# Retention followed by a gated MLP on one core: batch 0's states formed as 128x128 products of head pairs

## The chip, the core and the metric

The kernel runs on one NeuronCore of a Trainium2 chip. Its time is the device time of one execution in microseconds (us). Engines in the profile: PE is TensorE's matrix products and PEld its weight loads, DVE is VectorE, ACT is ScalarE, POOL is GpSimd, SP is SyncE, which here only issues DMAs. The profile also tells which share of TensorE's full clock was granted at each moment.

## The reference

Eight batches of eight heads, 576 positions, head dimension 64. Each head applies decaying causal attention without a softmax; the heads are laid side by side as 512 columns and go through two matrix products with a swish between them.

```python
# attention: q, k, v are (8, 8, 576, 64)
scores = scale * np.matmul(q, k.transpose(0, 1, 3, 2))
gamma = 1.0 - 2.0 ** (-5.0 - np.arange(H))
rel = pos[:, None] - pos[None, :]
Dmat = np.where(rel >= 0, gamma[:, None, None] ** rel, 0.0)
attn_out = np.matmul(scores * Dmat[None], v)
# MLP: x is (4608, 512), w_in (512, 2048), w_out (2048, 512)
x = attn_out.transpose(0, 2, 1, 3).reshape(B * S, H * D)
h = x @ w_in
g = h * (1.0 / (1.0 + np.exp(-beta * h)))
out = g @ w_out
```

## The kernel before

The decay is split into a factor on the queries (`gq`) and one on the values (`gv`, `gvh`), so a masked product of queries and keys remains, and what lies before a chunk of positions can be summed up in a state, the product of keys and values of each head, a 64x64 matrix. The first 512 positions of each batch are one block of the MLP; the last 64 positions of all batches together make another block. A block has "ups" (16 groups `fo` of 128 hidden columns, each the sum over four 128-row slices `ko` of `w_in`, then a swish on ACT that writes `gT`) and "downs" (four row groups `ms`, each the sum over 16 slices `fo` of `w_out`). Ups and downs of one block are products of 128x128 weights with 512 columns, 64 each. They are the list `fill`; attention steps of the next batch, loads and casts are put between its entries by `merged`, by hand-written positions in `streams`. The order of instructions on every engine is the order in which the program writes them (manual schedule).

Batch 0 is different, since nothing can run before it. It is loaded first (queries, keys, values, by head halves `a` and spans `s` of 256 positions), then `w_in` in pieces, then `w_out`, all in one queue on SP. Its steps are written out by hand at lines 718 to 773:

- `warm_up(n, cols)` puts n filler products on PE, on a tile of zeros in f32. In the profile each counts as two products.
- `t_q`, `s_T`: transposes of queries and keys on PE; `pre_q` (DVE) and `pre_s` (POOL) scale and cast ahead of them, and ACT copies the transposed keys to `kT`.
- `s_sc`: scores, then the causal mask on DVE (line 487).
- `s_st(a, n, s, rows)` (line 513): products of keys and values that make a state. States 0, 1 and 2 sum up what lies before positions 128, 256 and 384; the call at `n = 2` with the `high` rows of span 1 completes the state at the end of the block. Each head has a 64x64 product of its own; a product takes `rows` of one span, state 2 starts a PSUM tile of its own and forms span 0's part again.
- `s_keep(a, n, es)` (line 526) copies a state from PSUM to bf16 in `sbds`, the block-diagonal state of head pairs, on ACT for half 0 and mostly on DVE for half 1. The final state goes to `ends`.
- `s_O`, `s_cross`, `s_x`: masked scores times values; queries times state, added to the same PSUM tiles; the copy to `xT`, the input of the ups.

After line 773 the rest of half `a = 1` (`rest`: three `s_cross`, the last state's products, two `s_x`, casts of `w_in`) follows the first entry of `fill`, and `last_state` follows the third. Casts of `w_in` go to POOL and DVE (`cast_w_in`, line 209), those of `w_out` to DVE and ACT (`cast_w_out`, line 224).

Batch 1's queries and keys are transposed on PE among block 0's downs (`t_q`, `t_k`), after DVE's `pre_q` and POOL's `pre` have prepared them; later batches use DMA transposes (`turn`, line 330).

Of the kernel before, what the change touches and what calls it, by code (L numbers as in the profile page):

```python
# [19 lines left out]
def kernel(  # L20
# [218 lines left out]
    def warm_up(n, cols=256, tag="mm"):  # L239
        ph = psum.tile([P, MB], F32, name="ph", tag=tag, bufs=3 if tag == "mm" else 1)  # L240
        for _ in range(n):
            nc.tensor.matmul(ph[:, :cols], warm[:, :P], warm[:, :cols], start=True, stop=True,  # L242
                             skip_group_check=True)

    def betas():
        pb = psum.tile([P, FO], F32, name="pb", tag="mm", bufs=3)
# [79 lines left out]
    def heads(t, p):  # L326
        return t[:, 2 * p:2 * p + 2, :].rearrange("p h d -> p (h d)")
# [116 lines left out]
    def half(x):  # L444
        return slice(x * D, (x + 1) * D)
# [67 lines left out]
    def s_st(a, n, s, rows):  # L513

        if n not in s_sts:
            t = psum.tile([P, 1 if n > 1 else 2, 2, 2, D], F32, name="st", tag="mm" if n > 1 else "st", bufs=3 if n > 1 else 1)
            s_sts.update({2: t[:, 0]} if n > 1 else {0: t[:, 0], 1: t[:, 1]})
        S = spans[s]
        for i in range(2):
            for pl in range(2):  # L520
                for j in range(2):
                    h = 2 * (2 * a + pl) + j
                    nc.tensor.matmul(s_sts[n][half(j), a, pl, :], S["kn"][rows, i, h, :], S["vn"][rows, i, h, :],
                                     start=n != 1 and a == 0 and s == 0 and i == 0 and pl == 0, stop=True, skip_group_check=True)

    def s_keep(a, n, es):

        for j in range(2):
            if n < 3:
                es[j](sbds[n][half(j), 2 * a:2 * a + 2, half(j)], s_sts[n][half(j), a])  # L530
            else:
                es[j](ends[0][half(1 - j if a else j), 2 * a:2 * a + 2], s_sts[2][half(j), a])

    def piece(u, c):

# [139 lines left out]
    def down(m, ms, f0, fn=4, n0=0, nn=d_model):  # L675

        gT = gts[m]
        if f0 == 0:
            pos_[ms] = psum.tile([P, d_model], F32, name="po", tag="mm" if m or ms < 3 else "st", bufs=3 if m or ms < 3 else 1)
        po = pos_[ms]  # L680
        for fo in range(f0, f0 + fn):
            nc.tensor.matmul(po[:, :nn], gT[:, fo, ms, :], w_out_sb[:, fo, n0:n0 + nn],  # L682
                             start=(fo == 0), stop=(fo == FO - 1))
        if f0 + fn < FO:
            return
        if m not in ots:
            ots[m] = stage.tile([P, MB // P, d_model], F32, name="ot", tag="wt", bufs=4)
        ot = ots[m][:, ms, n0:n0 + nn]
        (nc.scalar.copy if m == 0 else nc.vector.tensor_copy)(ot, po[:, :nn])  # L689
        if m < B:  # L690
            rows = out[m * S:m * S + MB].rearrange("(s i) n -> s i n", i=CB)
            if m < 2:
                held.append((rows[:, ms, n0:n0 + nn], ot))
            else:
                nc.sync.dma_start(rows[:, ms, n0:n0 + nn], ot)
        else:
            for x in range(2):
                r0 = (2 * ms + x) * S + MB
                nc.sync.dma_start(out[r0:r0 + TL, n0:n0 + nn], ot[x * TL:(x + 1) * TL])
# [12 lines left out]
    def F(f, *a):  # L712
        return lambda: f(*a)
# [1 line left out]

    whole_span, low, high = slice(0, P), half(0), half(1)

    warm_up(5)
    betas()
    betas_safe()  # L720
    pre_q(0, 0)
# [1 line left out]
    t_q(0, 0)  # L723
    pre_q(0, 2)
    pre_q(0, 3)
    warm_up(1, 128)
    t_q(0, 1)
    warm_up(2, 128)
    pre_s(0, 0, 0)
    s_T(0, 0)  # L730
    pre_s(1, 0, 0)
    warm_up(2, 128)
    s_sc(0, 0, "sc")
    s_T(1, 0)
    pre_s(0, 0, 1)
    pre_s(1, 0, 1)
    warm_up(2, 128)
    s_T(0, 1)
    s_sc(1, 0, "mm")
    pre_s(0, 1, 0)  # L740
    pre_s(1, 1, 0)
    warm_up(2, 128, "st")
    s_T(1, 1)
    s_sc(0, 1, "sc")
    pre_s(0, 1, 1)
    pre_s(1, 1, 1)
    s_st(0, 0, 0, low)
    s_st(0, 1, 0, whole_span)
    s_keep(0, 0, (act, act))
    s_keep(0, 1, (act, act))  # L750
    s_st(0, 2, 0, whole_span)
    s_O(0, 0, "O")
    s_sc(1, 1, "mm")
    s_st(0, 2, 1, low)
    s_keep(0, 2, (act, act))
    s_O(1, 0, "O")
    s_cross(1, 0)
    s_cross(2, 0)
    s_x(0, 0, act)
    s_st(1, 0, 0, low)  # L760
    s_st(1, 1, 0, whole_span)
    s_keep(1, 0, (dve, dve))
    s_keep(1, 1, (dve, dve))
    s_O(0, 1, "sc")
    s_cross(3, 0)
    s_x(0, 1, act)
    s_st(1, 2, 0, whole_span)
    s_st(1, 2, 1, low)
    s_keep(1, 2, (act, act))
    s_O(1, 1, "sc")  # L770
    cast_w_in(0, (0, 1), (1,))
# [3 lines left out]
    def rest():  # L775
        for c in range(1, CB):
            s_cross(c, 1)
        for a in range(2):
            s_st(a, 2, 1, high)
        s_x(1, 0, act)  # L780
        s_x(1, 1, dve)
        cast_w_in(1, (2, 3))
        nc.vector.reciprocal(rbeta_sb[:], beta_sb[:])

    def last_state():
        for a in range(2):
# [35 lines left out]
    def triangles():  # L822
# [3 lines left out]
        for t, pattern in zip(tri, ([[1, CB], [CB, TL // CB]], [[1, TL]])):  # L826
            nc.gpsimd.memset(t[:], 1.0)
            for x in range(2):
# [1 line left out]
                nc.gpsimd.affine_select(out=t[w], in_=t[w], pattern=pattern, compare_op=ALU.is_ge,  # L830
                                        fill=0.0, base=0, channel_multiplier=-1)

    streams = [[(d0 + 2, F(triangles)), (1, rest), (3, F(last_state))], [(0, F(load_w_out, 0)), (1.6, F(cast_w_in, 2)), (2.1, F(cast_w_in, 3)), (2.2, F(load_w_out, 1)),
                (4.1, F(cast_w_in, 4)), (6.1, F(cast_w_in, 5)), (6.2, F(load_w_out, 2)), (8.1, F(cast_w_in, 6)),
                (10.1, F(cast_w_in, 7)), (10.2, F(load_w_out, 3))],
               [(d0 - 4 + 3.3 * g, F(cast_w_out, g)) for g in range(WG)],
# [100 lines left out]
```

## Time and profile before

| what | value |
|---|---|
| times of three executions | 299.07, 301.01 and 298.75 us, median 299.07 |
| the profiled execution | 300.7 us, of which the span from first to last instruction is 299.0 |
| TensorE's clock in the span, mean share granted | 0.993 |
| PE busy | 291.1 us (97%), 3309 products |
| DVE, ACT, POOL busy | 102.3, 145.4, 110.6 us |
| DMA | 53.99 MB, mean 181 GB/s |

Times in rows are in us unless marked ns. A timeline row holds the start, the length to the end of the last of the group, engine, line, operation, tiles and count, and in brackets the idle time of the engine before it and what ended that. In a row of the table of stretches, each engine has its busy time and, in brackets, the number of instructions that began there; after them come the granted clock and the DMA share. A product's recorded length contains its passage through the array, which overlaps with the next one's; what a product costs in a row of products is the distance of starts.

### The profile page before, as it was taken

What the parts mean: (1) busy time and instruction counts of PE and PEld (TensorE: products, weight loads), DVE (VectorE), ACT (ScalarE), POOL (GpSimd) and SP (SyncE); (2) the same over time, 40 slices, a digit from 0 to 9 for tenths busy, and PEclk for the clock granted to TensorE, in tenths of its full rate; (3) what the DMA queues carried; (4) which work ended last, traced back from release to release, by engine and by line L of the source; (5) the groups of instructions that cost most, each with busy time, mean ns of one, the idle gap of its engine ahead of it and who ended that gap; (6) DMA issues with size and microseconds to landing.
All of it is one profiled execution on the core that took longest, in us unless ns stands there. A gap on an engine that the chain in (4) does not pass through costs nothing.

```text
span 299.0 us, 7758 instructions
## 1 busy us (share of the span) xinstructions
PE 291.1 (97%) x3309; PEld 150.4 (50%) x3309; DVE 102.3 (34%) x214; ACT 145.4 (49%) x255; POOL 110.6 (37%) x219
## 2 busy tenths in 40 slices
PE   7969999999999999999999999999999999999996
PEld 5734446774454454455445544454454544444444
DVE  6727444713740353025402540255055400120012
ACT  5526817695257434843475248524771157107600
POOL 5947027855642802282229424865232000000000
PEclk9979999999999999999999999999999999999999
DMA  7999999999999959994989969999896110131012
GB/s 230 308 368 330 386 235 268 214 185 251 219 205 247 230 126 146 238 198 113 206 225 227 196 115 260 197 181 203 210 198 115 72 37 0 35 72 36 0 70 72
DMA packets 124178, 53.99 MB, mean 181 GB/s; under 512 B 101856, under 2 KB 116592, under 8 KB 124144
## 3 DMA queue, kind: packets, MB, share of 16 engines
q1 hardware_dynamic: 124112, 53.49, 80.8%
q8 instruction: 26, 0.43, 0.6%
q14 instruction: 8, 0.07, 0.1%
q10 hardware_dynamic: 32, 0.01, 0.0%
HBM read 36.71 MB, written 9.44 MB: 154 GB/s over the span
## 4 chain that ended last, share of the span: by engine, by line
PE 78%; DMA 9%; SPq 7%; POOL 3%; issue 2%; DVE 1%; ACT 0%; POOLq 0%
PE po L682 36%; PE ph L649 28%; PE ph L664 4%; DMA tln<-in_k_dram 4%; SPq L123 4%; DMA qn<-in_q_dram 4%; DMA kT<-kn 2%; SPq L330 1%; POOL qs L289 1%; SPq L96 1%; PE O L608 1%; PE st L580 1%; PE O L621 1%; POOL kn L311 1%; PE sc L562 1%
## 5 line engine op out<-in xcount | busy, mean ns | idle before, releaser
L682 PE MATMUL po<-w_out_sb,gT 128*128 128x512 bf16 (+2 forms) x608 | 128.8, 368 | 0.0
L651 ACT ACTIVATE gT<-ph,beta_sb 128x512 bf16<-128x512 f32 (+1 forms) x140 | 91.1, 656 | 52.0 <-PE ph L649 51.5
L649 PE MATMUL ph<-xT,w_in_sb 128*128 128x512 bf16 (+1 forms) x560 | 115.1, 364 | 0.0
L682 PEld LDWEIGHTS <-gT 128*128 128x128 bf16 x608 | 56.8, 98 | 63.0
L649 PEld LDWEIGHTS <-w_in_sb 128*128 128x128 bf16 x560 | 54.2, 98 | 57.7 <-DVE first L588 0.7
L689 DVE COPY ot<-po 128x512 f32<-128x512 f32 (+2 forms) x34 | 22.3, 657 | 72.1 <-PE po L682 72.0
L322 POOL CAST kn<-kvn 128x128 bf16<-128x128 f32 (+2 forms) x76 | 23.4, 344 | 47.9 <-DMA kvn<-in_k_dram 47.8
L289 POOL TENSOR_TENSOR qs<-qn,gq 128x256 bf16<-128x256 f32 (+1 forms) x36 | 26.3, 757 | 34.7 <-DMA qn<-in_q_dram 32.3
L569 DVE TENSOR_TENSOR R<-sc,tri 128x512 bf16<-128x512 f32 x28 | 17.4, 683 | 61.5 <-PE sc L562 61.5
L300 POOL TENSOR_TENSOR vn<-kvn,gv 128x512 bf16<-128x512 f32 x28 | 29.1, 1042 | 7.7 <-DMA kvn<-in_v_dram 7.5
L636 ACT CAST xT<-O 128x512 bf16<-128x512 f32 x14 | 7.5, 588 | 31.9 <-PE O L621 31.9
L591 ACT CAST sbd<-warm 128x256 bf16<-128x256 f32 x18 | 7.3, 405 | 25.5 <-DVE warm L588 20.6
L664 PE MATMUL ph<-xT,w_in_sb 128*128 128x512 bf16 x56 | 13.4, 397 | 0.0
L588 DVE TENSOR_TENSOR first<-st,warm 128x256 f32<-128x256 f32 x24 | 10.2, 425 | 2.5
L588 DVE TENSOR_TENSOR warm<-st,first 128x256 f32<-128x256 f32 x18 | 7.6, 422 | 9.6 <-PE st L580 8.4
L636 DVE CAST xT<-O 128x512 bf16<-128x512 f32 x14 | 9.0, 686 | 5.4 <-PE O L621 5.4
L667 ACT ACTIVATE gT<-ph,beta_sb 128x512 bf16<-128x512 f32 x14 | 8.5, 687 | 4.3 <-PE ph L664 4.2
L310 POOL TENSOR_TENSOR kn<-tln,gq 128x128 bf16<-128x128 f32 (+1 forms) x12 | 5.6, 470 | 12.8 <-DMA tln<-in_q_dram 9.1
L214 POOL CAST w_in_sb<-wt 128x256 bf16<-128x256 f32 (+1 forms) x15 | 7.7, 528 | 5.4 <-DMA wt<-in_moe_w_in_dram 5.2
L664 PEld LDWEIGHTS <-w_in_sb 128*128 128x128 bf16 x56 | 5.4, 100 | 6.7 <-issue 0.6
L242 PE MATMUL ph<-warm 128*128 128x128 f32 (+1 forms) x28 | 7.2, 396 | 1.3 <-DVE warm L135 1.3
L591 ACT CAST sbd<-first 128x256 bf16<-128x256 f32 x18 | 7.3, 405 | 2.3 <-DVE first L588 0.2
(105 smaller groups left out, 168.2 us busy)
## 6 DMA issues: line engine op xcount, KB each, us to landing
qn<-in_q_dram SPq DMA_DIRECT2D x16, 512.0 KB, 5.3
kvn<-in_k_dram SPq DMA_DIRECT2D x32, 256.0 KB, 5.9
kvn<-in_v_dram SPq DMA_DIRECT2D x32, 256.0 KB, 5.4
out_dram<-ot SPq DMA_DIRECT2D x31, 256.0 KB, 3.7
wt<-in_moe_w_out_dram SPq DMA_DIRECT2D x8, 512.0 KB, 7.4
wt<-in_moe_w_in_dram SPq DMA_DIRECT2D x5, 512.0 KB, 9.4
wt<-in_moe_w_in_dram SPq DMA_DIRECT2D x6, 256.0 KB, 6.9
out_dram<-ot SPq DMA_DIRECT2D x9, 128.0 KB, 2.4
```

The source lines that it names most:

```text
L289: nc.gpsimd.tensor_tensor(batch[b]["qs"][:, cs, to], q_tiles[b][:, hs, cs].rearrange("p h i d -> p i h d"), gq[:, cs, hs].unsqueeze(3).to_ ...
L300: nc.gpsimd.tensor_tensor(live[i]["vn"], kv_tiles.pop(i)[:, 1], gains(gv, c), ALU.mult)
L322: nc.gpsimd.tensor_copy(kn[:, c % 2, to], t[:, 0, hs])
L569: nc.vector.tensor_tensor(R[x][:, j].rearrange("k c p q -> k (c p) q"), sc[x, j].rearrange("k c p q -> k (c p) q"), mask, ALU.mult)
L588: nc.vector.tensor_tensor(new[:], add, sums[(c - 1) % 2][:], ALU.add)
L591: nc.scalar.copy((sbq[c] if c < NC - 1 else ends[u])[:], new[:])
L636: (nc.scalar.copy if n % 2 else nc.vector.tensor_copy)(x, o)
L649: nc.tensor.matmul(ph, w_in_sb[:, ko, fo * P:(fo + 1) * P], xts[m][:, ko, :, w], start=(ko == 0), stop=(ko == KO - 1))
L651: nc.scalar.activation(gts[m][:, fo, :, w], ph, ACT.Silu, scale=beta_sb[:, fo:fo + 1])
L664: nc.tensor.matmul(phs[f][:], w_in_sb[:, ko, f * P:(f + 1) * P], xts[m][:, ko], start=(ko == 0), stop=(ko == KO - 1))
L682: nc.tensor.matmul(po[:, :nn], gT[:, fo, ms, :], w_out_sb[:, fo, n0:n0 + nn], start=(fo == 0), stop=(fo == FO - 1))
L689: (nc.scalar.copy if m == 0 else nc.vector.tensor_copy)(ot, po[:, :nn])
```

## The change

- `warm_up` gains a form with 512 columns; the opening five fillers of 256 columns become two of 512 and one of 256.
- The nine later fillers (f32, 128 columns, at five places and one single) become five calls of `keep_warm`, one bf16 product of 512 columns each, of the identity with itself.
- `s_st` makes one 128x128 product for a pair of heads in place of two 64x64 ones; `s_keep` copies the two diagonal 64x64 squares out. States 1, 2 and the end of the block now grow in one PSUM tile (`s_sts[1]`): span 0 is taken in whole once, state 1 is copied, then span 1's low rows are added, state 2 is copied, then the high rows are added. State 0 keeps the tile tagged `st`. The call for state 1 now stands ahead of that for state 0.
- The last products move out of `rest` into `last_products` at position 2.5 of `fill`, and `last_state` moves from 3 to 3.6.
- In `down`, block 0's products from `fo` = 3 on are made as two products of 256 columns.

```diff
--- before.py
+++ after.py
@@ -239,8 +239,14 @@
     def warm_up(n, cols=256, tag="mm"):
         ph = psum.tile([P, MB], F32, name="ph", tag=tag, bufs=3 if tag == "mm" else 1)
         for _ in range(n):
-            nc.tensor.matmul(ph[:, :cols], warm[:, :P], warm[:, :cols], start=True, stop=True,
+            src = warm[:].unsqueeze(1).to_broadcast([P, 2, 256]) if cols > 256 else warm[:, :cols]
+            nc.tensor.matmul(ph[:, :cols], warm[:, :P], src, start=True, stop=True,
                              skip_group_check=True)
+
+    def keep_warm(tag="mm"):
+        ph = psum.tile([P, CB, P], F32, name="ph", tag=tag, bufs=3 if tag == "mm" else 1)
+        nc.tensor.matmul(ph[:], ident[:], ident[:].unsqueeze(1).to_broadcast([P, CB, P]), start=True, stop=True,
+                         skip_group_check=True)
 
     def betas():
         pb = psum.tile([P, FO], F32, name="pb", tag="mm", bufs=3)
@@ -513,23 +519,22 @@
     def s_st(a, n, s, rows):
 
         if n not in s_sts:
-            t = psum.tile([P, 1 if n > 1 else 2, 2, 2, D], F32, name="st", tag="mm" if n > 1 else "st", bufs=3 if n > 1 else 1)
-            s_sts.update({2: t[:, 0]} if n > 1 else {0: t[:, 0], 1: t[:, 1]})
+            s_sts[n] = psum.tile([P, HP, P], F32, name="st", tag="mm" if n else "st", bufs=3 if n else 1)
         S = spans[s]
         for i in range(2):
-            for pl in range(2):
-                for j in range(2):
-                    h = 2 * (2 * a + pl) + j
-                    nc.tensor.matmul(s_sts[n][half(j), a, pl, :], S["kn"][rows, i, h, :], S["vn"][rows, i, h, :],
-                                     start=n != 1 and a == 0 and s == 0 and i == 0 and pl == 0, stop=True, skip_group_check=True)
+            for p in (2 * a, 2 * a + 1):
+                nc.tensor.matmul(s_sts[n][:, p, :], heads(S["kn"][rows, i], p), heads(S["vn"][rows, i], p),
+                                 start=a == 0 and s == 0 and i == 0 and p == 0, stop=True, skip_group_check=True)
 
     def s_keep(a, n, es):
 
+        ps = slice(2 * a, 2 * a + 2)
         for j in range(2):
+            st = s_sts[min(n, 1)][half(j), ps, half(j)]
             if n < 3:
-                es[j](sbds[n][half(j), 2 * a:2 * a + 2, half(j)], s_sts[n][half(j), a])
+                es[j](sbds[n][half(j), ps, half(j)], st)
             else:
-                es[j](ends[0][half(1 - j if a else j), 2 * a:2 * a + 2], s_sts[2][half(j), a])
+                es[j](ends[0][half(1 - j if a else j), ps], st)
 
     def piece(u, c):
 
@@ -679,8 +684,10 @@
             pos_[ms] = psum.tile([P, d_model], F32, name="po", tag="mm" if m or ms < 3 else "st", bufs=3 if m or ms < 3 else 1)
         po = pos_[ms]
         for fo in range(f0, f0 + fn):
-            nc.tensor.matmul(po[:, :nn], gT[:, fo, ms, :], w_out_sb[:, fo, n0:n0 + nn],
-                             start=(fo == 0), stop=(fo == FO - 1))
+            parts = ((0, nn),) if m or fo < 3 else ((0, nn // 2), (nn // 2, nn))
+            for x, y in parts:
+                nc.tensor.matmul(po[:, x:y], gT[:, fo, ms, :], w_out_sb[:, fo, n0 + x:n0 + y],
+                                 start=(fo == 0), stop=(fo == FO - 1), skip_group_check=m == 0)
         if f0 + fn < FO:
             return
         if m not in ots:
@@ -715,7 +722,8 @@
 
     whole_span, low, high = slice(0, P), half(0), half(1)
 
-    warm_up(5)
+    warm_up(2, MB)
+    warm_up(1)
     betas()
     betas_safe()
     pre_q(0, 0)
@@ -723,49 +731,47 @@
     t_q(0, 0)
     pre_q(0, 2)
     pre_q(0, 3)
-    warm_up(1, 128)
+    keep_warm()
     t_q(0, 1)
-    warm_up(2, 128)
+    keep_warm()
     pre_s(0, 0, 0)
     s_T(0, 0)
     pre_s(1, 0, 0)
-    warm_up(2, 128)
+    keep_warm()
     s_sc(0, 0, "sc")
     s_T(1, 0)
     pre_s(0, 0, 1)
     pre_s(1, 0, 1)
-    warm_up(2, 128)
+    keep_warm()
     s_T(0, 1)
     s_sc(1, 0, "mm")
     pre_s(0, 1, 0)
     pre_s(1, 1, 0)
-    warm_up(2, 128, "st")
+    keep_warm("st")
     s_T(1, 1)
     s_sc(0, 1, "sc")
     pre_s(0, 1, 1)
     pre_s(1, 1, 1)
+    s_st(0, 1, 0, whole_span)
+    s_keep(0, 1, (act, act))
     s_st(0, 0, 0, low)
-    s_st(0, 1, 0, whole_span)
     s_keep(0, 0, (act, act))
-    s_keep(0, 1, (act, act))
-    s_st(0, 2, 0, whole_span)
     s_O(0, 0, "O")
     s_sc(1, 1, "mm")
-    s_st(0, 2, 1, low)
+    s_st(0, 1, 1, low)
     s_keep(0, 2, (act, act))
     s_O(1, 0, "O")
     s_cross(1, 0)
     s_cross(2, 0)
     s_x(0, 0, act)
+    s_st(1, 1, 0, whole_span)
+    s_keep(1, 1, (dve, dve))
     s_st(1, 0, 0, low)
-    s_st(1, 1, 0, whole_span)
     s_keep(1, 0, (dve, dve))
-    s_keep(1, 1, (dve, dve))
     s_O(0, 1, "sc")
     s_cross(3, 0)
     s_x(0, 1, act)
-    s_st(1, 2, 0, whole_span)
-    s_st(1, 2, 1, low)
+    s_st(1, 1, 1, low)
     s_keep(1, 2, (act, act))
     s_O(1, 1, "sc")
     cast_w_in(0, (0, 1), (1,))
@@ -775,12 +781,14 @@
     def rest():
         for c in range(1, CB):
             s_cross(c, 1)
-        for a in range(2):
-            s_st(a, 2, 1, high)
         s_x(1, 0, act)
         s_x(1, 1, dve)
         cast_w_in(1, (2, 3))
         nc.vector.reciprocal(rbeta_sb[:], beta_sb[:])
+
+    def last_products():
+        for a in range(2):
+            s_st(a, 1, 1, high)
 
     def last_state():
         for a in range(2):
@@ -830,7 +838,7 @@
                 nc.gpsimd.affine_select(out=t[w], in_=t[w], pattern=pattern, compare_op=ALU.is_ge,
                                         fill=0.0, base=0, channel_multiplier=-1)
 
-    streams = [[(d0 + 2, F(triangles)), (1, rest), (3, F(last_state))], [(0, F(load_w_out, 0)), (1.6, F(cast_w_in, 2)), (2.1, F(cast_w_in, 3)), (2.2, F(load_w_out, 1)),
+    streams = [[(d0 + 2, F(triangles)), (1, rest), (2.5, F(last_products)), (3.6, F(last_state))], [(0, F(load_w_out, 0)), (1.6, F(cast_w_in, 2)), (2.1, F(cast_w_in, 3)), (2.2, F(load_w_out, 1)),
                 (4.1, F(cast_w_in, 4)), (6.1, F(cast_w_in, 5)), (6.2, F(load_w_out, 2)), (8.1, F(cast_w_in, 6)),
                 (10.1, F(cast_w_in, 7)), (10.2, F(load_w_out, 3))],
                [(d0 - 4 + 3.3 * g, F(cast_w_out, g)) for g in range(WG)],
```

## The prediction

> **What bounds the kernel now.** I read the page first, then the waits of PE, a table of stretches, and the timelines of the first 60 us.
>
> ```profile
> PE 291.1 (97%) x3309; PEld 150.4 (50%) x3309; DVE 102.3 (34%) x214; ACT 145.4 (49%) x255; POOL 110.6 (37%) x219
> PEclk9979999999999999999999999999999999999999
> q8 instruction: 26, 0.43, 0.6%
> ...
> PE O L498 <- issue: 2.4, 1, 2.4
> PE sc L562 <- DMA kT<-kn: 0.3, 1, 0.3
> ...
> 177.46 0.70 DVE ot L689
> 225.31 4.87 DMA kT<-kn
> ```
>
> PE is busy 97% of the span, so time can come from three places only: fewer or cheaper products, PE's idle time, or its clock. Of the idle time one wait stands out: 2.4 us before line 498, put down to "issue", which is a wait that the profile cannot name. The clock row dips in one slice, the one from 15 to 22 us. The chain that ended last runs over DMAs between 177 and 225 us, but it gets there from an output copy behind PE's downs, and PE waited only 0.3 us at its end: that stretch moves with PE.
>
> ```profile
> 14.81 0.41 PE L498 MATMUL O<-R,vn 64*64 64x128 bf16 x14
> 17.62 0.24 PE L498 MATMUL O<-R,vn 64*64 64x128 bf16 x2 [2.40 <-issue]
> 19.04 1.89 PE L664 MATMUL ph<-xT,w_in_sb 128*128 128x512 bf16 x4
> 20.72 0.85 PE L506 MATMUL O<-qT,sbd 128*128 128x128 bf16 x6
> ...
> 0.00:12.12 12.12, 9.92 (x94) 7.67 (x94) 7.40 (x23) 6.28 (x11) 8.39 (x26) 1.00 0.93 253
> 0.00:15.22 15.22, 13.02 (x223) 10.14 (x223) 10.50 (x28) 9.01 (x19) 11.39 (x31) 1.00 0.97 271
> 18.20:21.60 3.40, 3.40 (x46) 1.89 (x42) 0.00 (x0) 1.23 (x4) 1.61 (x5) 0.50 1.08 385
> ...
> q8 instruction: 1, 0.02, 6.0%
> ```
>
> The gap lies inside one group: 14 of 16 like products run, two come 2.4 us later, with operands long there. I read it as a wait for PE's own program. The page's queue q8 moved 26 packets, 0.43 MB, so 16.5 KB each; PE ran 3309 products and 3309 weight loads, 6618 instructions, 255 for a packet. The last row is the DMA view of 15.0 to 16.2 us, with the first packet of all; to 15 us there is none. At 15.22 us, 223 products and as many loads had begun: 446 instructions. So PE began with two packets in hand less some 66 instructions of start-up (2 x 256 - 446), and asked for the third on entering the second, at instruction 190, product 95. By the row to 12.12 us, 94 had begun by then. From 12.1 to 17.6 us the packet took **5.5 us**, on DMA engines at a share of 0.93 to 1.08. PE used the 256 instructions in 3.1 us, and stood still for the rest.
>
> The clock follows: from 18.2 to 21.6 us the granted share is 0.50. Four products of 512 columns take 1.68 us there (19.04 to 20.72), 0.42 each. The stretch costs half of 3.4 us, 1.7. That also sorts the times shown: 301.01 and the profiled 300.7 lie 1.6 to 2.3 above 299.07 and 298.75, the size of one such stretch. I take it that the wait is in every execution and the half clock in some.
>
> **The change, part by part.**
>
> ```profile
> L242 PE MATMUL ph<-warm 128*128 128x128 f32 (+1 forms) x28 | 7.2, 396 | 1.3 <-DVE warm L135 1.3
> L523 PE MATMUL st<-vn,kn 64*64 64x64 bf16 (+1 forms) x80 | 2.7, 203 | 0.0
> 7.92 0.66 PE L242 MATMUL ph<-warm 128*128 128x128 f32 x4
> 8.42 0.39 PE L468 MATMUL T<-ident,kn 128*128 128x128 bf16 x4
> 12.37 0.66 PE L523 MATMUL st<-vn,kn 64*64 64x64 bf16 x24
> 12.96 0.42 PE L498 MATMUL O<-R,vn 64*64 64x128 bf16 x16
> 50.02 0.40 PE L431 MATMUL st<-vn,kn 128*128 128x128 bf16 x4
> 50.26 1.03 PE L682 MATMUL po<-w_out_sb,gT 128*128 128x512 bf16 x4
> ```
>
> *The wait.* Fillers fall from 28 counted products to 11 (two of 512 and one of 256 columns count double, five single), states from 80 to 32. In the new order the 95th product is in the first state call and the 223rd in `last_products`, behind 12 products of 512 columns and six `s_cross`. I put the ask at 12.2 us, so the packet is there at 17.7, and the 223rd due near 19.2 (below). The wait goes: **-2.4**. Bounds: 0 if the packet is as late again as it was needed, -2.4 if it is early. I take the end, with 1.5 us of margin.
>
> *The half clock.* PE has no gap over a microsecond left, so the stretch should not recur: **-1.7** in an execution that had it, 0 in one that had not.
>
> *State products.* Before, 24 took 0.59 us (12.37 to 12.96). Whole pairs cost what line 431 shows, four in 0.24. The 32 new ones then cost 1.9 us and the 80 old ones 2.0: nothing on PE, and a gain in instructions alone.
>
> *Fillers.* An f32 four cost 0.50 (7.92 to 8.42); a bf16 one of 512 columns 0.22 (27.96 less 26.23 over eight, in rows further down). The five places fall from 2.1 to 1.1 us, but PE is paced by others there.
>
> ```profile
> 10.02 5.05 DVE L487 TENSOR_TENSOR R<-sc,causal 128x512 bf16<-128x512 f32 x8 [1.20 <-PE sc L484]
> 14.98 1.21 DVE L530 CAST sbd<-st 64x128 bf16<-64x128 f32 x4
> 11.00 2.04 POOL L461 TENSOR_TENSOR vn<-kvn,gvh 128x512 bf16<-128x512 f32 x2
> 14.64 0.58 ACT L510 CAST xT<-O 128x512 bf16<-128x512 f32 x1
> ```
>
> POOL's values of span 0 end near 12.04 whatever PE does, and eight masks run on DVE without a break. Only their start comes earlier, by the 0.25 that the first filler gives up before `s_T(0, 0)`: the masks end at 14.8 in place of 15.07.
>
> *The new wait.* State 2 is now added into the tile that `s_keep(1, 1)` reads, on DVE behind the masks: two copies of 0.3 end at 15.4. PE waits 0.7 us ahead of that product, and `s_O(1, 1)` and the first ups stand behind it, until 15.7 and 15.95. Without the program wait the old order would have had its ups at 16.2, behind ACT's `xT` copy (0.58, after the `s_cross` at 15.4). So the wait hides behind what was there, and a net **-0.15** remains. Bounds: -0.4, +0.7.
>
> *What the ups then meet.* First ups 15.95; `s_cross` to 17.2; second ups to 18.0; their `xT` half at 18.05; third ups to 19.0; last products 0.45; fourth to 20.3; eight more products to 22.0; 8 (lines 649) to 23.7; the 32 of line 664 follow. All need weights:
>
> ```profile
> 22.22 0.75 POOL L214 CAST w_in_sb<-wt 128x512 bf16<-128x512 f32 x1 [0.60 <-DMA wt<-in_moe_w_in_dram]
> 23.77 0.61 POOL L214 CAST w_in_sb<-wt 128x512 bf16<-128x512 f32 x1 [0.80 <-DMA wt<-in_moe_w_in_dram]
> 25.02 2.18 POOL L214 CAST w_in_sb<-wt 128x512 bf16<-128x512 f32 x2 [0.64 <-DMA wt<-in_moe_w_in_dram]
> 26.23 1.89 PE L649 MATMUL ph<-xT,w_in_sb 128*128 128x512 bf16 x8
> 27.96 7.07 PE L664 MATMUL ph<-xT,w_in_sb 128*128 128x512 bf16 x32
> 34.87 3.40 PE L682 MATMUL po<-w_out_sb,gT 128*128 128x512 bf16 x15
> ```
>
> The piece that gates the 32 is cast at 22.97, 0.7 ahead; the next at 24.4 and 27.2 for uses at 25.4 and 28.9. So the casts, which wait for DMA, still hide, and the downs start at 30.6 in place of 34.87: 4.25 earlier in the profiled execution.
>
> *Halves.* Of block 0's 64 down products 52 are split.
>
> ```profile
> 58.48 5.84 PE L649 MATMUL ph<-xT,w_in_sb 128*128 128x256 bf16 x52
> 41.11 1.30 DVE L292 TENSOR_TENSOR qs<-qn,gq 128x512 bf16<-128x512 f32 x2 [0.28 <-DMA qn<-in_q_dram]
> 42.15 0.73 POOL L322 CAST kn<-kvn 128x512 bf16<-128x512 f32 x1 [12.56 <-DMA kvn<-in_k_dram]
> 46.54 0.61 PE L346 MATMUL T<-ident,qs 128*128 128x128 bf16 x8
> 46.99 0.39 PE L352 MATMUL T<-ident,kn 128*128 128x128 bf16 x4
> 109.26:110.40 1.14, 1.14 (x131) 1.14 (x133) 0.06 (x1) 0.00 (x0) 0.00 (x0) 1.00 0.87 160
> 0.00:109.26 109.26, 104.66 (x1177) 59.13 (x1177) 51.31 (x116) 60.39 (x115) 58.37 (x117) 0.98 1.04 255
> ```
>
> 52 products of 256 columns take 5.84 us with 0.16 of tail, so 0.109 apart; two make 0.218 against 0.216: **+0.1**, bounds 0 and +0.3 (0.112 with the tail). What they do is to the program: 17 fillers and 48 state products fewer, 52 halves more, 13 products fewer in all. Packet borders lie every 128 products, at 128n - 33, so behind block 0 each falls 13 products later in the work. That matters in a burst like the one at 109.26, 131 products in 1.14 us: a packet that began and ended in it would be used up in 1.1 us. The border nearest is product 1119 + 13 = 1132, against the burst's 1177 to 1308; the next is 1260. Each packet spans some 8 us of work. No new wait.
>
> *The lid.* Batch 1's queries are ready on DVE at 42.41 and its first keys on POOL at 42.88, both behind DMAs that PE doesn't drive. PE uses them at 46.54 and 46.99, so PE can come 4.1 us earlier and no more.
>
> **The sum**, on the profiled execution: 300.7 - 2.4 - 1.7 - 0.15 + 0.1 = 296.55, just under the lid (300.7 - 4.1 = 296.6). Against the median, whose execution I take to have had no half clock: 299.07 - 2.45 = 296.6. Both meet at **296.6 us**.
>
> A rule that speaks against the first step: the Trainium skill, page Runtime: NRT & Kernel Launch, section Instruction fetch mechanics, gives PE room for 2048 instructions, refilled in blocks of 256, and calls the cost of a border mostly hidden. By it PE would not run dry after 446, and the sum would be without the 2.4, 299.0. The trace agrees with its block, 255 a packet, and not with the 2048.
>
> **The rivals.**
>
> 1. *The whole 4.1 counts against the median.* If the half clock was in all executions and the 1.6 us to the median is only profiling, 299.07 - 4.1 = 295.0. For it: the wait of 2.4 us is itself always there. Against: 301.01 was not profiled. Chance 0.20.
> 2. *The wait stays or moves.* If the 2.4 us are not the program's, or the packet comes as late at product 223, only 0.05 to 1.3 us are left as gain: 298 to 299.0, say 298.5. For it: "issue" names nothing; a second packet in as saturated a DMA might take longer. Against: the packet's place, and 446. The Trainium skill's rule on 2048 instructions is this case. Chance 0.10.
> 3. *Thinner fillers lose the clock.* PE's filler time from 7.9 to 12.1 halves; if that lets the clock fall for one stretch of 3.4 us, up to 1.7 are lost: 298.3. Against: DVE and POOL pace PE there, so part would hide, and other products continue. Chance 0.05.
> 4. *Slower: borders fall into the bursts.* If the shift is not 13 products but 45 to 70 (counted differently, or the halves not kept as two), borders near 1119, 1503, 1887 and 2271 fall to the start of the four bursts at 109, 139, 169 and 200 us. Each then uses a packet in 1.1 us that takes 3 to 5.5 to come: four waits of 2 to 4.4, some +12, 308.6. It decides from a shift of about 35. Against: my count is 13. Chance 0.07.
>
> **How the numbers follow.** The forecast holds 0.58, with a range of its own from 295.9 to 297.8 (the bounds of the new wait and the halves; nothing below the lid but 0.7 for what other executions' DMAs allow). A measurement of this kernel can tell about 1% from no change, so 296.08 is the border of faster. A quarter of the forecast's chance lies under it, 0.15, with rival 1's 0.20: **0.35 faster**. Slower is rival 4, **0.07**; the rest, **0.58**, is within 1%. For 8 in 10 the range reaches down to rival 1 and up over rivals 2 and 3: **294.8 to 298.7**.
>
> **What would show it.** Right: no wait of PE at line 498; the clock at 1.00 from 5 us on; the first instruction packet still near 15 us with PE working through 17.6; the first ups near 16 and the first downs near 30.6; a short wait ahead of the state product for span 1's low rows at `a = 1`; transposes of batch 1 close behind POOL's casts, at 43.0. Wrong: an "issue" wait at another place, above all in the bursts; a clock of 0.5 in the first 15 us; downs at 30.6 but transposes of batch 1 waiting for DMA by more than 0.5 us, which would mean a tighter lid.

## The result, and the profile after

The changed kernel takes **298.44 us** (median of 14 executions, 297.69 to 299.03). The kernel before, run beside it 14 times, takes 300.53 (298.75 to 302.35). The ratio is 0.9929, with an interval of 0.9909 to 0.9949: 0.7% faster, inside the 1% that the prediction called no change. A ratio leaves out executions more than 1.5% above the fastest of their kernel, which medians and ranges keep. The profiled execution takes 298.38 us, its span 296.6; before these were 300.7 and 299.0.

The page of the changed kernel (some 30 product records are missing from its trace, so that 3268 products stand beside 3296 weight loads):

```profile
span 296.6 us, 7705 instructions
PE 286.4 (97%) x3268; PEld 151.8 (51%) x3296; DVE 102.9 (35%) x214; ACT 145.6 (49%) x255; POOL 110.8 (37%) x219
PEclk9999999999999999999999999999999999999999
```

The dip of the clock row is gone. The waits of PE in the changed kernel (total, number of times, longest):

```profile
PE po L689 <- issue: 2.1, 13, 0.2
...
PE sc L567 <- DMA kT<-kn: 1.0, 1, 1.0
```

There is no wait at the `s_O` line (now 504) any more. The row of 13 times 0.2 comes from the missing records: the first run with the queries sooner in experiment 6, whose trace lacks none, has no such row. The wait for the last keys is new in size: 0.3 before, 1.0 now. PE's timeline of the changed kernel, the rows that answer to those of before:

```profile
12.07 0.71 PE L526 MATMUL st<-vn,kn 128*128 128x128 bf16 x8 [0.20 <-POOL vn L467]
12.71 0.42 PE L504 MATMUL O<-R,vn 64*64 64x128 bf16 x16
...
14.95 0.42 PE L504 MATMUL O<-R,vn 64*64 64x128 bf16 x16
15.30 0.28 PE L512 MATMUL O<-qT,sbd 128*128 128x128 bf16 x2
15.52 0.39 PE L526 MATMUL st<-vn,kn 64*128 64x128 bf16 x4
15.84 0.42 PE L504 MATMUL O<-R,vn 64*64 64x128 bf16 x16
16.26 1.02 PE L669 MATMUL ph<-xT,w_in_sb 128*128 128x512 bf16 x3
...
31.23 10.62 PE L689 MATMUL po<-w_out_sb,gT 128*128 128x512 bf16 x84
41.69 0.61 PE L352 MATMUL T<-ident,qs 128*128 128x128 bf16 x8
```

Batch 1's first transposes in the kernel before:

```profile
45.23 0.61 PE L346 MATMUL T<-ident,qs 128*128 128x128 bf16 x8
```

PE now works without a stop through the time at which it stood still before; the ups begin at 16.26 instead of 19.04, the downs at 31.23 instead of 34.87. So **3.6 us** are won by then, and batch 1's transposes still stand 3.54 earlier (41.69 against 45.23). But the span is only 2.4 shorter. The rest is given back at two places, both far from the change. The first is at the last keys; PE's timeline before, then after:

```profile
216.64 0.78 PE L562 MATMUL sc<-qT,kT 64*64 64x64 bf16 x64
230.23 0.32 PE L562 MATMUL sc<-kT 64*64 64x64 bf16 x16 [0.34 <-DMA kT<-kn]
```

```profile
212.93 0.88 PE L567 MATMUL sc<-qT,kT 64*64 64x64 bf16 x64
227.16 0.32 PE L567 MATMUL sc<-kT 64*64 64x64 bf16 x16 [0.97 <-DMA kT<-kn]
```

At the scores of the batch before, PE is 3.71 ahead; behind the wait for the last `kT` it is 3.07 ahead, so **0.64** is lost there. That is the size in this one execution: in a second profile of the changed kernel, in experiment 6, the wait is 0.42 and only 0.06 is lost. The second place is behind the last product. The changed kernel's timeline of SP's queue from 292.2 us (both issues in one row), and from 293.85 us (the last alone):

```profile
292.42 1.88 SPq L702 DMA_DIRECT2D out_dram<-ot  x2
...
293.91 0.38 SPq L702 DMA_DIRECT2D out_dram<-ot  x1
```

Its timeline of DVE, the last copy:

```profile
292.99 0.29 DVE L696 COPY ot<-po 128x128 f32<-128x128 f32 x1 [0.60 <-PE po L689]
```

And the row of the instruction queue in its DMA view from 291.9 to 293.6 us (queue, packets, MB, share of the engines):

```profile
q8 instruction: 1, 0.02, 5.0%
```

The last copy is done at 293.28, but SP issues its DMA only at 293.91, since the issue before it, at 292.42, occupied SP's queue for 1.4 us where the neighbouring ones took 0.33 to 0.38. In that window a packet of PE's program moved (start 292.10, 1.35 us by its record). The end comes **0.66** later than the last product would have it: 3.62 us behind that product's end, 2.96 before. This stretch behind the last product is called the tail below.

### The profile page after: what moved, and what is told of

It reads as the page before. It is cut to its first block, busy times and chain, and to the rows that moved or that the text cites. A ratio compares the mean times of both kernels' runs of the same rounds, so it can differ in the third digit from the quotient of the medians.

```text
span 296.6 us, 7705 instructions
## 1 busy us (share of the span) xinstructions
PE 286.4 (97%) x3268; PEld 151.8 (51%) x3296; DVE 102.9 (35%) x214; ACT 145.6 (49%) x255; POOL 110.8 (37%) x219
## 4 chain that ended last, share of the span: by engine, by line
PE 76%; SPq 9%; DMA 9%; POOL 4%; issue 2%; DVE 0%; POOLq 0%
PE po L689 35%; PE ph L654 29%; SPq L123 5%; PE ph L669 4%; DMA tln<-in_k_dram 3%; DMA kvn<-in_k_dram 2%; DMA qn<-in_q_dram 2%; SPq L336 2%; DMA kT<-kn 2%; PE O L613 1%; PE st L585 1%; SPq L96 1%; POOL qs L295 1%; PE O L626 1%; PE sc L567 1%
## 5 line engine op out<-in xcount | busy, mean ns | idle before, releaser
L689 PE MATMUL po<-w_out_sb,gT 128*128 128x512 bf16 (+2 forms) x644 | 125.8, 351 | 2.2 <-issue 2.1
L689 PEld LDWEIGHTS <-gT 128*128 128x128 bf16 x660 | 62.0, 98 | 59.0
L669 PE MATMUL ph<-xT,w_in_sb 128*128 128x512 bf16 x54 | 12.8, 379 | 0.1
L231 DVE TENSOR_SCALAR w_out_sb<-wt,rbeta_sb 128x512 bf16<-128x512 f32 x13 | 5.9, 485 | 5.0 <-DMA wt<-in_moe_w_out_dram 5.0
```

Source lines behind the costliest of these rows:

```text
L669: nc.tensor.matmul(phs[f][:], w_in_sb[:, ko, f * P:(f + 1) * P], xts[m][:, ko], start=(ko == 0), stop=(ko == KO - 1))
L689: nc.tensor.matmul(po[:, x:y], gT[:, fo, ms, :], w_out_sb[:, fo, n0 + x:n0 + y], start=(fo == 0), stop=(fo == FO - 1), skip_group_check=m ...
```

## The experiments

They ran in three groups. Each group ran on one chip, beside runs of the kernel before of its own: 300.51 us in the first group, 300.70 in the second, 300.05 in the third (medians of 19, 31 and 35 executions). Products are counted from the start of the program; a packet border lies near product 128n - 33, as the prediction has it, and the last paragraph of experiment 4 makes this exact.

**1. Is the wait PE's program? The count moved earlier, with no part of the change.** In the kernel before, two fillers give way to 84 small products of zeros.

```diff
-    warm_up(5)
+    warm_up(3)
+    little(84)     # 84 products 64x64, of a bf16 tile of zeros
```

> The kernel before, with nothing of the change: of its five opening fillers two (counted as four products) make room for 84 products of 64x64 on zeros, so 80 more products stand ahead of all work of batch 0, and every packet border falls 80 products earlier in it. Program-packet theory: the third packet is asked for at product 95, now near 6.5 us, and is there by 12; product 223 is now the old 143rd, due near 13, so the wait at line 498 is gone. The fourth packet is asked for near 13 and there near 18.5; product 351 is the old 271st, the last state's products ahead of the second ups, due near 17.5: a wait of 0 to 1.3 us there. The clock stays at 1.00 after its start. Time 297.5 to 299 us, as the changed kernel's, without one of its edits. Rival, the gap belongs to the work at line 498 or to a time near 15 us: it stays, with the half clock, and the time is 300.5 us.

Measured: 298.62 us, ratio 0.9921 (0.9886 to 0.9956). The wait in this kernel's waits of PE:

```profile
PE st L532 <- issue: 0.7, 1, 0.7
```

Its stretch from the start up to the wait:

```profile
0.00:18.21 18.21, 16.41 (x351) 12.97 (x351) 11.60 (x33) 10.26 (x23) 12.49 (x35) 1.00 1.00 278
```

And the row of its PE timeline in which the work goes on:

```profile
18.89 0.41 PE L532 MATMUL st<-vn,kn 64*64 64x64 bf16 x14 [0.68 <-issue]
```

The wait at line 498 is gone, though that code stands as before, and the first packet moves at 9.92 us instead of 15. A smaller wait appears elsewhere, with 351 products and 351 loads begun: 223 + 128, exactly one packet on. This is what separates the program from any wait that hangs on data or on the time, and it earns the kernel before 0.8% with none of the change's parts.

**2. The fillers alone.** The kernel before, with the bf16 fillers.

```diff
-    warm_up(5)
+    warm_up(2, MB)
+    warm_up(1)
...
-    warm_up(1, 128)    # and the four calls of two
+    keep_warm()
```

> The kernel before with the bf16 fillers alone (28 counted filler products become 11). Program-packet theory: the border at product 223 moves 17 products on in the work, so the wait leaves line 498 and stands among the state products of line 523 or thereabouts, 2.0 to 2.3 us long, followed by the half clock; later borders 17 products later fall into no burst; time 299.8 to 300.8 us. Rival, the wait belongs to the work at line 498 (an operand, a semaphore): it stays there with 2.4 us. Rival, thinner fillers lose the clock: a share of 0.5 in a stretch before 15 us, up to 1.7 us more than before.

Measured: 300.80 us, ratio 0.9991 (0.9952 to 1.003); the profiled execution was the longest of the ten, 303.77. The wait in this kernel's waits of PE:

```profile
PE st L529 <- issue: 2.7, 1, 2.7
```

Its stretch from the start up to the wait, and a later one:

```profile
0.00:15.88 15.88, 13.51 (x223) 8.13 (x223) 10.78 (x30) 9.33 (x20) 11.90 (x33) 1.00 0.97 271
20.80:24.20 3.40, 3.40 (x28) 1.82 (x27) 2.40 (x9) 0.58 (x1) 2.02 (x4) 0.50 1.03 371
```

The wait stands on another line, behind exactly 223 products again: the program's border has not moved, only the product that lies on it. Fewer filler instructions by themselves buy nothing.

**3. The states alone.** The kernel before, with the states as pair products and the later last products; fillers as before, downs whole.

```diff
-            for pl in range(2):
-                for j in range(2):
-                    ... st of one head, 64x64
+            for p in (2 * a, 2 * a + 1):
+                ... st of a pair, 128x128
```

> The kernel before with the states as products of head pairs in the new order and with the later last products, but with the old fillers and whole downs: 48 products fewer in front. Program-packet theory: product 223 is the fourth of the first ups, due near 17.0 us, so the wait shrinks to 0.5 to 1.0 us and stands there, and the clock stays at 1.00; later borders fall 48 products later than before, at the start of the bursts near 138, 168 and 198 us (a packet in 1.1 to 1.8 us) and near it at 108 (3.5 us): 2 to 3 us of wait in each of three, 6 to 8 us in all; time 303 to 306 us. Rival, the gain comes from the state products themselves: 298.4 us, no later waits.

Measured: **297.89 us**, ratio 0.9906 (0.987 to 0.9941). All of PE's waits in this kernel:

```profile
PE ph L242 <- DVE warm L135: 1.3, 1, 1.3
PE T L346 <- DVE qs L292: 0.6, 3, 0.2
PE sc L484 <- ACT kT L469: 0.2, 1, 0.2
```

Its first 15.9 us:

```profile
0.00:15.90 15.90, 13.76 (x198) 10.45 (x199) 10.86 (x29) 9.02 (x19) 12.06 (x32) 1.00 0.97 270
```

No "issue" wait is left at all. By 15.9 us only 198 products have begun, 25 short of the border, and the first packet moves at 15.11. My expectation of later waits, and of 303 to 306 us, was wrong: in the last two bursts near 167 and 197 us a border lies only 2 and 8 products behind the start, and PE got through without a wait in this execution. This one part is worth the whole change.

**4. The halves alone, and the change without them.** The first is the kernel before with the split downs, the second the changed kernel with this line:

```diff
-            parts = ((0, nn),) if m or fo < 3 else ((0, nn // 2), (nn // 2, nn))
+            parts = ((0, nn),)
```

> The kernel before with the column halves alone. Program-packet theory: nothing changes up to block 0's downs, so the wait of 2.4 us at line 498 and the half clock stay; later borders fall 52 products earlier than before, which puts them at the start of the bursts near 109 and 140 us (a packet used in 1.1 to 1.5 us) and close to it near 81 and 171 us (2.8 and 3.2 us): about 2.5 us of wait in each of the first two and about 1 in the others, 5 to 8 us in all, 306 to 308 us. Rival, the halves are only a cost: 300.6 us.

> The changed kernel without the column halves: 52 products fewer ahead of block 1, so each later packet border falls 52 products further on than in the changed kernel, 65 further than before. Program-packet theory: the front end stays as in the changed kernel (no wait near 15 us, clock 1.00), but three bursts, near 106, 136 and 166 us, use a whole packet in about 1.1 us, and a fourth near 197 us one in 2.7; PE waits some 2 to 3 us in each of the three and up to 1.5 in the fourth: 6 to 9 us in all, about 305 to 307 us. Rival, the halves are only a cost: 0.1 us less than the changed kernel, 298.3 us, and no wait of PE above 1.1 us.

Measured: halves alone **308.75 us**, ratio 1.0259 (1.0216 to 1.0303); the change without halves 303.02, ratio 1.006 (1.0029 to 1.009). Waits of PE with the halves alone:

```profile
PE O L621 <- issue: 3.7, 2, 3.4
PE po L684 <- issue: 2.0, 1, 2.0
PE O L498 <- issue: 2.0, 1, 2.0
```

A row of its PE timeline, behind the longest of them:

```profile
145.03 0.21 PE L621 MATMUL O<-qT,sbd 64*64 64x64 bf16 x1 [3.35 <-issue]
```

And its stretch from there:

```profile
144.90:148.40 3.50, 3.37 (x9) 1.28 (x10) 2.30 (x5) 1.62 (x4) 1.91 (x4) 0.57 1.11 157
```

Waits of PE in the change without the halves:

```profile
PE O L626 <- issue: 2.2, 1, 2.2
PE po L689 <- issue: 1.8, 1, 1.8
```

These are rival 4's waits in the bursts, at 141.7 and 178.8 us in the one kernel, 167.7 and 201.5 in the other. Behind the first of them the clock was halved for 3.4 us. So the halves are there for the count: the other parts take 65 products away, which puts borders 18 and 25 products into two bursts, and 52 halves put them back. The halves alone lose, and so does the change without them; together the two shifts cancel. Without halves the waits add up to 4.0 us, where I had expected 6 to 9: two bursts wait and two do not. The halves alone lost a little more than the 306 to 308 us that I had expected.

All of these waits, the 0.4 us one at 110.8 included, stand on a border, though products alone put it up to four early. Besides products and weight loads, the traces hold 16 other instructions of PE, spread over the whole program. With these counted, each of the ten "issue" waits in the traces of before and of the experiments, those of the 13-fold row aside, stands behind exactly 256m - 63 instructions, m from 2 to 19. That is the plainest sign that packets of 256 instructions make them.

**5. Do the fillers hold the clock?** The changed kernel without its five `keep_warm` calls.

> The changed kernel without its five bf16 fillers; only the opening ones stay. If the fillers are needed for the clock, the granted share falls to 0.5 for one or two stretches of 3.4 us between 8 and 15 us and the time rises by 0.5 to 1.7 us, to 299 to 300 us. If they are not, the clock stays at 1.00 and the time is the changed kernel's within 0.3 us, 298.1 to 298.7. Packet borders fall 5 products later than in the changed kernel, which puts none 18 products or more into a burst: no issue wait above 0.5 us.

Measured: 302.12 us, ratio 1.0005 (0.9951 to 1.006), ten executions between 297.76 and 304.83. The clock row of this kernel's page:

```profile
PEclk9659999999999999999999999999999999999999
```

Two of its stretches, the second inside the first:

```profile
10.26:23.90 13.64, 13.39 (x169) 8.19 (x167) 7.93 (x19) 5.45 (x14) 9.21 (x18) 0.50 1.09 350
11.40:14.80 3.40, 3.40 (x76) 2.47 (x70) 2.62 (x5) 1.88 (x6) 3.40 (x6) 0.50 1.13 323
```

Half the clock for 13.6 us in the profiled execution, though PE counts as busy for all of 11.40 to 14.80, and for the whole of the step of the clock from 13.67 to 17.08. In two executions of the ten the clock held; those took 297.76 and 299.01. The loss is larger than the 299 to 300 us that I expected, since the half clock lasted four steps and not one or two. So some filler is needed, and the short bf16 form is enough.

**6. The loss at the last keys.** The loads of the last batch's queries are issued two entries sooner in the changed kernel, so that SP's queue is past them when the keys' turn comes. The second run adds the same for keys and values (`7` to `9`, `5` to `7`).

```diff
-            sooner = 4 if b == B - 1 else 0
+            sooner = 6 if b == B - 1 else 0
```

> The changed kernel with the last batch's query loads written two places earlier in the list, ahead of an output copy that the DMA queue on SP waits for (1.1 us of its issues move forward). Theory that the last stretch from 174 to 225 us is a chain through SP's queue: PE's wait for the last key transposes (1.0 us in the changed kernel) falls to 0.3 or less and the median to 297.4 to 297.9. Rival, that wait is set by how long the DMAs take to land, or by something after them: it stays within 0.3 us and the time at 298.4.

> The changed kernel with the last batch's query loads two places sooner, again, to set it against the changed kernel on one chip: 0.5 to 0.8 us under it, 297.5 to 297.9 us. If the first run of it only had the better chip: within 0.2 us of it.

> As the run before, with the last batch's key and value loads two places sooner as well. If SP's queue is still the bound of the last stretch, a further 0.2 to 0.5 us less; PE's last wait for key transposes was gone already, so by the theory that this wait was all that the queue cost it makes no difference: within 0.2 us of the run with the queries alone.

> The changed kernel once more, beside the three that follow on one chip: 298.2 to 298.7 us, with a wait of 0.3 to 1.2 us for the last key transposes.

Measured: 297.74 us in the second group (ratio 0.9903, 0.9871 to 0.9934); in the third 297.83 (0.9937, 0.9908 to 0.9966), with the keys sooner too 297.70 (0.9948, 0.9919 to 0.9978), beside the changed kernel unaltered at 298.44 (0.9958, 0.993 to 0.9987). All of PE's waits with the queries sooner, in the third group:

```profile
PE po L689 <- issue: 2.1, 13, 0.2
PE ph L243 <- DVE warm L135: 1.3, 1, 1.3
PE sc L490 <- ACT kT L475: 0.7, 2, 0.5
PE T L352 <- DVE qs L298: 0.2, 1, 0.2
```

The wait for `kT` is no longer listed, and 0.6 us come back. In the same group the changed kernel unaltered had this wait:

```profile
PE sc L567 <- DMA kT<-kn: 0.4, 1, 0.4
```

So the wait was 0.4 in one profile of the changed kernel and 1.0 in the other, and the gain lies between the two. Moving the keys as well adds nothing that shows.

**7. The states alone with the queries sooner; states and halves with the old fillers.** The first is experiment 3's kernel with `sooner = 6`, the second the changed kernel with the f32 fillers of before.

> The state products alone (as in the run of that name: old fillers, whole downs) with the last batch's query loads two places earlier. If both gains add, about 0.7 us under the states alone: 297.0 to 297.4 us, no issue wait above 0.5 us and the last wait for key transposes at 0.3 us or less. If the queue is not the bound: 297.9.

> The changed kernel with the old f32 fillers: what the bf16 fillers are worth when the states and the halves stay. Borders fall 4 products earlier than before, into no burst by 18 products or more; product 223 is the fourth of the first ups as in the states alone, where no wait was left. If the bf16 fillers earn time (0.25 us earlier masks on DVE), it is 0.2 to 0.5 us slower than the changed kernel; if they earn nothing, the same, 298.0 to 298.6; the clock at 1.00 either way.

Measured: 297.68 us (ratio 0.9908, 0.9874 to 0.9942) and **297.50** (0.9921, 0.989 to 0.9952). The first is no better than experiment 3, so the two gains do not add: there was no `kT` wait left to take away. Its profile, of the longest of its ten executions (298.75), shows a wait at a border near 199 us:

```profile
PE O L620 <- issue: 0.9, 1, 0.9
```

PE's instructions are those of experiment 3, where the same border, 8 products into a burst, made no wait. So the whole downs lie close to the edge. The second is the fastest kernel of the third group, 0.94 below the changed kernel; neither case of my expectation had it faster. Two rows of its PE timeline:

```profile
31.82 10.62 PE L683 MATMUL po<-w_out_sb,gT 128*128 128x512 bf16 x84
...
226.25 0.74 PE L561 MATMUL sc<-kT 64*64 64x64 bf16 x64
```

Its SP queue, the last two issues:

```profile
291.93 0.33 SPq L696 DMA_DIRECT2D out_dram<-ot  x1
...
292.82 0.33 SPq L696 DMA_DIRECT2D out_dram<-ot  x1
```

Its DMA view from 291.9 to 293.6 us, all queues that moved anything:

```profile
q1 hardware_dynamic: 288, 0.20, 35.0%
```

Its downs begin 0.6 later than the changed kernel's (31.82 against 31.23), so the short fillers do earn something in front. But it has no wait at the last keys, and no instruction packet moves in the last window: its last one moved at 289.83 us, because 17 more products ahead put every border earlier in the work. Both last issues take 0.33, and the tail is 2.95 us.

The fourteen profiles agree in this. In five (the changed kernel, its second run, both runs with the queries sooner, the one with the keys sooner) the last packet begins 0.8 to 0.9 us before PE's last product ends, just as the last two output DMAs are due; an issue takes 1.2 to 1.45 us and the tail is 3.4 to 3.7. In the other eight experiments, and before, the packet begins at least 1.5 us ahead, and the tail is 2.9 to 3.0. In the five, the long issue ends 0.33 to 0.37 us behind the end of the packet's record. The same is seen within the traces: this kernel's issue at 262.58 takes 1.05 us where those at 259.12 and 266.03 take 0.59, and it ends 0.37 behind a packet. But a packet alone is not enough: in the kernel before, an issue at 294.73 takes 0.33 while a packet moves from 294.50 to 295.44. So the packet holds up some issues and not others; what decides it is not shown, and a run that moves the last packet and nothing else was not made. Nor was this kernel run with the queries sooner: its trace shows no wait at the last keys that could be taken away.

## Why the prediction was right in kind, and 1.8 us short

Forecast 296.6 with a range of 294.8 to 298.7; measured 298.44, within 1% of before, the case that held 0.58. It lies only 0.26 inside the upper end of the range, outside the 295.9 to 297.8 of the forecast's own steps, and beside rival 2's 298.5, though not for rival 2's reason. By its own steps:

- **The wait.** Right: gone, and experiments 1 and 2 show its cause at the very counts, 223 and 351. The packet's record ends at 16.60 and PE comes to product 223 near 19.6; behind the ten waits it went on 1.3 to 1.5 us after that end, so the margin was about the 1.5 us that I gave it. Two figures were not exact: the 66 instructions of start-up are 63, and a packet holds 256 instructions, not 255, as experiment 4's count shows (dividing all of PE's instructions by 26 packets left out the two in hand). That PE asks on entering the packet before is not shown either: in the states alone a packet began over 4 us ahead of that (130.48 against 135.18). The Trainium skill's 2048 instructions (page Runtime: NRT & Kernel Launch, section Instruction fetch mechanics), rival 2's rule, do not hold here; the same section's remark that the instruction memory is only two cache lines fits the counts, at the 256 instructions that it gives for a block.
- **The half clock.** Gone, as said. That it comes in some executions only was right as well, but there were more of them than I took from three times. Of the 31 executions of before in the second group, 7 had a mean clock of 0.998 or more (298.39 to 300.15 us), 16 had 0.993 or 0.994 (median near 300.7) and 8 had 0.987 to 0.989 (near 302.3): steps of some 1.5 us, one or two stretches. The median shown, 299.07, was by its time an execution without; the median of many is one with. Most of the gain in the medians is this: the changed kernel keeps its clock at 0.998 or above in all 14. So it is partly luck that the medians fell by 2.1, near the 2.5 of the forecast: I had put the half clock at nothing against the median, and the 2.45 of the other steps came only in small part.
- **The front (-0.15, and 4.25 by the downs).** Mis-sized by 0.6: the downs came 3.64 earlier. The step that failed is the price of the state products, for the 0.31 by which the first ups came late (16.26 in place of 15.95). I took line 431's 0.24 for four everywhere; but where a call has whole and half pairs, or follows another shape, it is dearer: the eight products at 12.07 take 0.64 to the next row. In the trace the starts are 0.056 apart within a shape and 0.15 from the last 128x128 product to the first of 64 rows. These steps lie ahead of `s_O(0, 1)`, which so came at 14.95; behind it are `s_cross` and ACT's `xT` copy, which ends at 16.21, just ahead of the ups. The other 0.3 is added by the third ups, which wait for DVE's `xT` half (done at 18.35, forecast 18.05) and start at 18.49, and by the last products, whose row takes 0.55 and not 0.45.
- **The new wait (0.7, hidden).** Right that it hides: DVE's copies end where I had them, but PE reached the product so late that no wait shows. DVE's row in the changed kernel:

```profile
14.79 1.21 DVE L535 CAST sbd<-st 64x128 bf16<-64x128 f32 x4
```

  The first two copies end at 15.4. The product follows at 15.52, 0.15 behind the start of the one before it, which is what a change of shape takes.
- **The halves (+0.1).** Right: 3.64 at the downs, 3.54 at the transposes.
- **The lid.** Not reached: batch 1's keys were used at 43.45.
- **"That stretch moves with PE", and the count past the bursts.** The step that failed. I priced everything behind batch 1 at nothing. Two things there do not move with PE: the DMA chain to the last keys came only some 3 us earlier (0.64 lost in the profiled execution), and the last packet border, moved 13 products later by my own count, came to lie on the output DMAs at the end (0.66 lost, with the cause as far as experiment 7 shows it). I had looked for borders in the bursts alone.

In the profiled executions the span fell by 2.41 where 4.15 was forecast. The three shortfalls, 0.61 + 0.64 + 0.66, less 0.17 that came back between 41.7 and 212.9 us (3.54 ahead there, 3.71 here), are the missing 1.74.

- **Rival 4** did not happen, but the reason that I gave for it is not exact. What counts is how many products of a burst lie ahead of a border, since the next border is 128 products on. In the four large bursts of experiments 3 and 4, borders 2 to 10 products in made no wait, one at 14 made 0.4 us, those at 18 to 29 made 1.8 to 3.4, and one at 36 none. It is no sharp line, as the 0.9 at 8 in experiment 7 shows. Taking the halves away makes rival 4's shift, 65 products; it brought two waits with 4.0 us in all, not four with 12.

At equal clock little is left. In the third group the executions of before with a clock of 0.998 or more, 15 of 35, have a median of 298.65, only 0.2 above the changed kernel's 298.44; the forecast had 2.45 there, and the 1.74 missing in the profiles would leave 0.7. The kernel with the states and halves, which loses nothing at the end, lies 1.15 below those executions. What stays open is whether the wait itself is shorter in executions that keep the clock, since each trace of before is of one execution, and that one had the half clock.

## What to carry to other kernels

When the trace puts a wait down to nothing, count the instructions of that engine up to it, and move the count without moving the work: 84 idle products in front told the cause apart from every data wait. After an edit that changes the number of instructions, follow every later packet border through dense stretches of small instructions and to the last output transfers, not only the stretch that was edited. And take the baseline from many executions: a time that comes in steps of 1.5 us has a median that three values don't show.

## What the runs showed of the hardware

- PE ran dry only at packet borders: after 446 products and weight loads, one packet of 256 instructions later with 80 more products in front, and at later borders inside bursts. Waits took 0.4 to 3.4 us. In all ten, PE went on 1.3 to 1.5 us behind the end of the packet's record (before: 16.18 to 17.62), which itself lasts 0.9 to 1.7 us.
- Gaps of PE of 2.0 to 2.4 us were followed by half the clock in some executions (before; halves alone at 15.5 us, half clock from 19.07 to 22.49) and not in others (1.8 and 2.2 us without halves, clock 1.000; in six of the ten executions of that kernel the clock was 0.994 or less). The Trainium skill, page TensorE: Matmul & The Clock Gate, section Why this matters for your kernels, warns of gaps above some 3 us; here shorter ones were enough. Stretches lasted 3.41 us or a multiple (6.83 with the fillers alone, 13.65 without fillers).
- A PE that counts as busy for the whole of a 3.4 us stretch can still be held at half clock (76 products there, without fillers).
- A change of shape between products costs PE some 0.1 us (starts 0.15 apart in place of 0.056).
- The issue of an output DMA beside an instruction packet can take 1.2 to 1.45 us in place of 0.33 and then ends some 0.35 us behind the packet; other issues beside a packet take their usual time.
